# Attention over channels and a routed expert layer on one core: batch 1's k'q moved beside the expert blocks, the first block one step earlier

## The chip, the cores and the metric

The kernel runs on 1 core of a Trainium2 chip. The metric is the device time of one execution in microseconds (us). A core has five engines with instruction queues of their own: TensorE (PE, its weight loads listed as PEld), VectorE (DVE), ScalarE (ACT), GpSimd (POOL) and SyncE (SP, which here issues the loads). The order on each queue is fixed when the program is built.

## The reference

```python
def _attn_ref(q, k, v, tau):              # q, k, v: 4 x 5056 x 256, float32
    qn = q / (np.linalg.norm(q, axis=1, keepdims=True) + 1e-06)
    kn = k / (np.linalg.norm(k, axis=1, keepdims=True) + 1e-06)
    s = kn.transpose(0, 2, 1) @ qn / tau  # 256 x 256 for each batch
    a = softmax of s along its last axis
    return v @ a

def _moe_ref(x, modality_id, w_gate, modality_bias, w1, w2):   # x: 20224 x 256
    logits = x @ w_gate + modality_bias[modality_id]           # 8 experts
    e_idx = np.argmax(logits, axis=1)
    gate_w = softmax(logits) at e_idx
    for e in range(8):
        mask = e_idx == e
        h = np.maximum(x[mask] @ w1[e], 0.0)                   # 256 to 1024
        out[mask] = gate_w[mask, None] * (h @ w2[e])           # 1024 to 256
```

The attention's output, read as 20224 tokens of 256 numbers, is the input of the expert layer. With the reference's inputs three of the eight experts get all tokens: 8704, 1408 and 10112, which are 17, 3 and 20 blocks of 512 rows or less.

## The kernel before

**Stages and steps.** A batch is cut into NS = 10 steps of 512 tokens (the last one is 448). For each batch the kernel first forms the 256 x 256 product k'q and the sums of squares of q and k over all tokens (`kq_pieces`), then the softmax (`softmax_pieces`), then, step by step, v times the attention matrix, the routing, and a scatter of the rows into a DRAM buffer `xs` sorted by expert (`va_pieces`). Blocks of 512 rows of one expert are loaded from `xs` and go through the two expert matrices (`block_pieces`). Batch 0's k'q runs alone at the start. After that there is one loop over g = 0 to 39 (four batches of ten steps). In step g the kernel traces, interleaved piece by piece (`_interleave`): one expert block, if one is due; the v work of step g and the v transposes of step g + 1; and one step of the next batch's k'q.

**k'q.** A step of `kq_pieces` loads 512 rows of q and of k, splits each into a high and a low part (a cast on ACT and a subtraction on DVE, lines 257 and 258) and multiplies: for each of 4 row groups and 2 halves of k's columns a 512-column and a 256-column matmul (lines 283 and 287). The sums of squares come in one of two ways. For steps in the table `SELF` (line 73) TensorE multiplies the part by itself (line 294, tile `selfk` or `selfq`) and the diagonal is taken at the end (line 306, `dg`). For the others ACT squares the rows (line 272) and DVE adds them to `acc` (line 274). Batch 1 has k in `SELF` for steps 0 to 3 and q for none.

**v work and routing.** `tr` transposes v on TensorE (line 460, `vtp`) and splits it (464, 465). `av` does 24 matmuls for each step (line 476, `xp`), and ACT copies the results to `x` (line 480). `route` is a chain of small DVE operations (lines 485 to 533) with three small matmuls in it (`rp`, lines 512 to 514). It yields row numbers `pi`, and POOL issues four scatters for each step (line 407).

**Blocks.** After step g, `slots_by(g)` says how many blocks have been picked. `pick` (a chain of DVE operations on one row) takes an expert with at least 512 rows that are not taken yet. With START = 3 the first pick follows step 3. A block picked after step g runs in step g + LAG, LAG = 4, so the first one runs in step 7. Its weights (w1r and w2r, four loads of 512 KB for each block, lines 615 and 619) wait for the pick, and its rows (`xr`, line 596) for the landing of all scatters up to the step of the pick. Four pieces prepare a block at the end of the step before it: two weight splits (ACT line 634, DVE line 635) and two transposes of its rows (line 645, `xtp`, split by 650 and 651). Then come `hp` matmuls (line 663), the split of h (668, 669) and `y` matmuls (line 683). 40 blocks are run, 33 of them in steps 7 to 39 and the rest after the loop.

**Buffers.** PSUM has eight banks: y0, y1, g0, g1, two `h` and two `aux`. Before the first block (`early`), v's transposes use an `h` bank and y1, and the routing's small matmuls y0. `selfk` and `selfq` hold an `h` bank each while they accumulate. Batch 0's k'q accumulates in y0 and y1. In batch 1, steps 2 to 4 of q and k are loaded into buffers of the expert weights (tags w1r, w2r), the other steps into two buffers of their own.

**Order.** The Tile framework puts the instructions on the queues. It takes priorities from the order in which pieces are traced and uses durations of its own, so that on an engine with nothing due it can place ready work of a much later step. `setup_bias(b)`, traced at the middle of the batch before, is an example: it has a load `modi` on SP behind a memset on POOL (lines 182 and 186).

Of the kernel before, what the change touches and what calls it, by code (L numbers as in the profile page):

```python
# [8 lines left out]
F32 = mybir.dt.float32  # L9
# [9 lines left out]

def _interleave(*streams):  # L20

    lists = [list(s) for s in streams if s]
    total = [len(x) for x in lists]
    at = [0] * len(lists)
    while any(a < n for a, n in zip(at, total)):
        i = min(
            (i for i in range(len(lists)) if at[i] < total[i]),
            key=lambda i: ((at[i] + 0.5) / total[i], i),
        )
        lists[i][at[i]]()  # L30
        at[i] += 1
# [3 lines left out]
def kernel(  # L35
# [14 lines left out]
    P = 128  # L50
    B, N, C = q.shape
    T, D = out.shape
    E, _, FF = w1.shape
    TT = 4
    STEP = P * TT
    NS = -(-N // STEP)
# [14 lines left out]
    LAG = 4  # L71

    SELF = {
        "q": [{1, 4, 7}, set(), set(), set()],
        "k": [set(range(NS)), set(range(4)), set(), set()],
    }
    START = 3

    def parts(s):
        return P if s < NS - 1 else PL  # L80
# [137 lines left out]
    def kq_pieces(b, s):  # L218
        pp = parts(s)
        st = {}  # L220
        t0 = s * STEP

        def load():
            if s == 0:
                gram[b] = [
                    ps1.tile([P, 2 * C], F32, tag=f"{'y' if b == 0 else 'g'}{m}", name=f"g{m}_{b}")
                    for m in range(CH)
                ]
                acc[b] = p1.tile([P, 2, 2 * C], F32, tag="acc", name=f"acc_{b}", bufs=2)
                for n in ("k", "q"):  # L230
                    if SELF[n][b]:
                        selfp[n, b] = ps2.tile([P, CH, 2 * P], F32, tag="h", name=f"self{n}_{b}")
                        norm[n, b] = p1.tile([P, CH], F32, tag=f"n{n}", name=f"n{n}_{b}")
            for n, src, tag in (("q", q, "w1r"), ("k", k, "w2r")):
                if (b == 0 and s % 5 >= 2) or (b == 1 and 2 <= s < START + 2):
                    st[n] = p3.tile([P, TT, C], F32, tag=tag, name=f"{n}_{b}_{s}")
                else:
                    st[n] = p2.tile([P, TT, C], F32, tag=n, name=f"{n}_{b}_{s}")
                rows = src[b, t0 : t0 + pp * TT, :].rearrange("(p t) c -> p t c", t=TT)
                if b == 0 and s == 0:  # L240
                    st[n + "rows"] = rows
                else:
                    nc.sync.dma_start(st[n][:pp], rows)
            if b == 0 and s == 0:
                for h in range(2):
                    ts = slice(2 * h, 2 * h + 2)
                    for n in ("q", "k"):
                        nc.sync.dma_start(st[n][:, ts, :], st[n + "rows"][:, ts, :])

        def split(h):  # L250
            ts = slice(2 * h, 2 * h + 2)
            more = h == 1 and (b == 0 or (b == 1 and s < START + 1))
            qs = p2.tile([P, 2, 2 * C], F32R, tag="xh" if more else "qs", name=f"qs_{b}_{s}_{h}")
            ks = p2.tile([P, 2, 2 * C], F32R, tag="xl" if more else "ks", name=f"ks_{b}_{s}_{h}")
            st[h] = (qs, ks)
            for n, t in (("q", qs), ("k", ks)):
                nc.scalar.copy(t[:pp, :, 0:C], st[n][:pp, ts, :])  # L257
                nc.vector.tensor_tensor(  # L258
                    t[:pp, :, C : 2 * C], st[n][:pp, ts, :], t[:pp, :, 0:C].bitcast(F32), ALU.subtract
                )  # L260
            a = acc[b]
            for n, o in (("q", 0), ("k", C)):
                if s in SELF[n][b]:
                    continue
                first = h == 0 and s == min(set(range(NS)) - SELF[n][b])
                sq = a[:, :, o : o + C]
                if not first:
                    if b == 0 or (b == 1 and s < START + 1):
                        sq = p3.tile([P, 2, C], F32, tag="hh" if n == "q" else "hl", name=f"sq_{b}_{s}_{h}_{n}")
                    else:  # L270
                        sq = p2.tile([P, 2, C], F32, tag="sq", name=f"sq_{b}_{s}_{h}_{n}")
                nc.scalar.activation(sq[:pp], st[n][:pp, ts, :], AF.Square)
                if not first:
                    nc.vector.tensor_tensor(a[:pp, :, o : o + C], a[:pp, :, o : o + C], sq[:pp], ALU.add)  # L274

        def mm(h):
            qs, ks = st[h]
            for t in range(2):
                first = s == 0 and h == 0 and t == 0
                last = s == NS - 1 and h == 1 and t == 1  # L280
                for m in range(CH):
                    g = gram[b][m]
                    nc.tensor.matmul(  # L283
                        g, ks[:pp, t, m * P : (m + 1) * P], qs[:pp, t, :],
                        start=first, stop=False, skip_group_check=True,
                    )
                    nc.tensor.matmul(  # L287
                        g[:, 0:C], ks[:pp, t, C + m * P : C + (m + 1) * P], qs[:pp, t, 0:C],
                        start=False, stop=last, skip_group_check=True,
                    )  # L290
                    for n, x in (("k", ks), ("q", qs)):
                        mine = SELF[n][b]
                        if s in mine:
                            nc.tensor.matmul(  # L294
                                selfp[n, b][:, m, :], x[:pp, t, m * P : (m + 1) * P],
                                x[:pp, t, :].rearrange("p (s c) -> p s c", s=2)[:, :, m * P : (m + 1) * P],
                                start=s == min(mine) and h == 0 and t == 0 and m == 0,
                                stop=s == max(mine) and h == 1 and t == 1,
                                skip_group_check=True,
                            )  # L300
            for n in ("k", "q"):
                if h == 1 and SELF[n][b] and s == max(SELF[n][b]):

                    dg = p1.tile([P, 2 * P], F32, tag="sc", name=f"dg{n}_{b}", bufs=2)
                    for m in range(CH):
                        nc.vector.scalar_tensor_tensor(
                            dg, selfp[n, b][:, m, :], 1.0, ident12, ALU.mult, ALU.mult,
                            accum_out=norm[n, b][:, m : m + 1],
                        )

        yield load
        for h in range(2):
            yield lambda h=h: split(h)
            yield lambda h=h: mm(h)
# [109 lines left out]

    def slots_by(g):

        return max(0, g + 1 - START)

    first_block = LAG + START

    def va_pieces(b, s):
# [20 lines left out]
            st["L"] = p2.tile([P, TT, E], F32, tag="L", name=f"L_{g}")  # L452

        def tr(h):
            if early and h == 1:
                tp = ps1.tile([P, 512], F32, tag="y1", name=f"vtp_{g}_{h}")
            else:
                tp = ps2.tile([P, 512], F32, tag="h" if early else "aux", name=f"vtp_{g}_{h}")
            for t in range(TT):
                nc.tensor.matmul(  # L460
                    tp[:, t * P : (t + 1) * P], st["v"][:, t, h * P : (h + 1) * P], ident,
                    is_transpose=True, start=t == 0, stop=True, skip_group_check=True,
                )
            nc.scalar.copy(st["vh"][:, h, :], tp)
            nc.vector.tensor_tensor(st["vl"][:, h, :], tp, st["vh"][:, h, :].bitcast(F32), ALU.subtract)
# [16 lines left out]
        def route():  # L482
# [22 lines left out]
            ohf = oh.rearrange("p e t -> p (e t)")  # L505
            rtf = run_t.rearrange("p e t -> p (e t)")
            nc.vector.tensor_tensor_scan(rtf, keep, ohf, 0.0, ALU.mult, ALU.add)
            if early:
                rp = ps1.tile([P, 512], F32, tag="y0", name=f"rp_{g}")
            else:  # L510
                rp = ps2.tile([P, 512], F32, tag="aux", name=f"rp_{g}")
# [256 lines left out]
    for g in range(G):  # L768
        b, s = divmod(g, NS)
        streams = []  # L770
        for gg, blk in waiting:
            if gg <= g - LAG + 1:
                once(blk, "load")
        if len(waiting) > 0 and waiting[0][0] <= g - LAG:
            _, blk = waiting.pop(0)
            streams.append(block_stream(blk, waiting[0][1] if waiting and waiting[0][0] <= g - LAG + 1 else None))
        soft = list(softmax_pieces(b)) if s == 0 and b > 0 else []
        streams.append(soft + (va[g + 1][0] if g + 1 < G else []) + va[g][1])
        if b + 1 < B:
            streams.append(list(kq_pieces(b + 1, s)))  # L780
        _interleave(*streams)
        if waiting and waiting[0][0] <= g - LAG + 1:
            once(waiting[0][1], "load")
            once(waiting[0][1], "prep")
        if s == NS // 2 and b + 1 < B:
# [98 lines left out]
```

## Time and profile before

| | us |
|---|---|
| median of 3 runs (range) | 1244.78 (1243.62 to 1246.61) |
| the profiled execution's own time | 1245.85 |
| its span, first to last instruction | 1243.5 |
| PE busy | 1221.7 |
| DVE busy | 843.9 |
| ACT busy | 754.1 |
| POOL busy | 348.7 |

The page gives the busy time of each engine and the chain of work that ended last. For one stretch, the trace is read by windows (busy time of each engine between two moments) and by rows in order of time: start in us, length in us, engine, line, operation, output and input, shapes, count; in brackets the idle time before the row and what ended it. A matmul's length holds its way through the array, so what one costs in a row of many is the distance from its start to the next start. "SPq" is the queue that issues loads.

### The profile page before, as it was taken

Reading aid. Unit: us, or ns where it says so; the run is one execution under the profiler, and the core shown is the slowest. Engines: PE = TensorE matmul, PEld = TensorE weight load, DVE = VectorE, ACT = ScalarE, POOL = GpSimd, SP = SyncE. Lnnn points to the kernel's source line nnn. Section 1 sums busy time; section 2 is a strip of 40 time slices with the busy share of each in tenths; the row PEclk is TensorE's granted clock in tenths of the full one; section 3 lists DMA queues with packets and bytes.
Section 4 is the critical chain, followed back from the end, with each engine's and each line's share of the span. In section 5 each row is a group of like instructions: output and inputs, shape, how many; then the busy total and the mean of one; then the engine's idle time right before and its main releaser. Section 6 shows DMA issues by size and latency. Waiting matters only on the chain.

```text
span 1243.5 us, 23786 instructions
## 1 busy us (share of the span) xinstructions
PE 1221.7 (98%) x8316; PEld 1116.2 (90%) x8316; DVE 843.9 (68%) x2215; ACT 754.1 (61%) x1531; POOL 348.7 (28%) x348
## 2 busy tenths in 40 slices
PE   8998999999999999999999999999999999999997
PEld 6897899999999999999999999999999999999997
DVE  7898967777777666866776776566655666665552
ACT  7885866666666666766666665565555555545553
POOL 0036343132222222322222222222332222321121
PEclk9998999999999999999999999999999999999999
DMA  9758864555555555555555554444554443467320
GB/s 322 252 191 282 271 205 151 161 190 186 176 170 172 178 171 171 162 176 170 170 181 186 175 167 136 136 134 143 164 173 154 149 153 121 147 211 219 119 95 28
DMA packets 113026, 215.06 MB, mean 173 GB/s; under 512 B 16128, under 2 KB 61696, under 8 KB 112896
## 3 DMA queue, kind: packets, MB, share of 16 engines
q1 hardware_dynamic: 97632, 171.84, 44.3%
q0 software_dynamic: 15264, 41.60, 8.8%
q8 instruction: 67, 1.10, 0.4%
q14 instruction: 63, 0.52, 0.1%
HBM read 167.06 MB, written 46.34 MB: 172 GB/s over the span
## 4 chain that ended last, share of the span: by engine, by line
PE 90%; DVE 3%; issue 3%; DMA 2%; ACT 1%; POOL 1%; SPq 0%; POOLq 0%; DVEq 0%; ACTq 0%
PE y L683 33%; PE hp L663 33%; PE xp L476 9%; PE g L283 5%; PE g L287 3%; PE vtp L460 3%; PE xtp L645 2%; DMA q<-in_q_dram 1%; PE selfk L294 1%; DVE acc L274 1%; POOL out_dram L407 1%; DMA xs<-x,pi 0%; PE ns L329 0%; DVE qs L258 0%; DVE w2l L635 0%
## 5 line engine op out<-in xcount | busy, mean ns | idle before, releaser
L683 PE MATMUL y<-w2h,hh 128*128 128x256 f32 x1264 | 356.7, 282 | 0.0
L407 POOL DMA_INDIRECT xs<-x,pi x160 | 173.0, 1081 | 647.8 <-ACT w1h L634 483.2
L683 PE MATMUL y<-w2l,hh 128*128 128x256 f32 x1264 | 352.7, 279 | 0.0
L683 PE MATMUL y<-w2h,hl 128*128 128x256 f32 x1264 | 351.4, 278 | 0.0
L669 DVE SCALAR_TENSOR_TENSOR hl<-hp,hh 128x512 fp32r<-128x512 f32 (+1 forms) x320 | 216.2, 676 | 147.0 <-ACT hh L668 146.8
L668 ACT ACTIVATE hh<-hp 128x512 fp32r<-128x512 f32 (+1 forms) x320 | 190.1, 594 | 169.2 <-PE hp L663 167.2
L663 PE MATMUL hp<-xh,w1h 128*128 128x512 f32 (+1 forms) x640 | 255.8, 400 | 0.3 <-ACT xh L650 0.3
L663 PE MATMUL hp<-xl,w1h 128*128 128x512 f32 (+1 forms) x640 | 250.3, 391 | 0.0
L663 PE MATMUL hp<-xh,w1l 128*128 128x512 f32 (+1 forms) x640 | 249.7, 390 | 0.0
L683 PEld LDWEIGHTS y<-w2h,hh 128*128 128x128 f32 x1264 | 237.5, 188 | 12.0 <-ACT yo L694 0.2
L683 PEld LDWEIGHTS y<-w2l,hh 128*128 128x128 f32 x1264 | 238.1, 188 | 10.0
L683 PEld LDWEIGHTS y<-w2h,hl 128*128 128x128 f32 x1264 | 236.6, 187 | 0.1
L407 POOL DMA_INDIRECT out_dram<-yo,xr x158 | 163.0, 1032 | 157.5 <-ACT yo L694 113.3
L635 DVE TENSOR_TENSOR w2l<-w2r,w2h 128x512 fp32r<-128x512 f32 x160 | 110.2, 689 | 71.9 <-ACT w2h L634 71.9
L635 DVE TENSOR_TENSOR w1l<-w1r,w1h 128x512 fp32r<-128x512 f32 x160 | 109.8, 686 | 55.5 <-ACT w1h L634 55.1
L634 ACT CAST w2h<-w2r 128x512 fp32r<-128x512 f32 x160 | 100.1, 625 | 74.9 <-PE y L683 67.4
L663 PEld LDWEIGHTS hp<-xh,w1l 128*128 128x128 f32 x640 | 120.1, 188 | 26.2
L634 ACT CAST w1h<-w1r 128x512 fp32r<-128x512 f32 x160 | 101.0, 631 | 60.0 <-PE hp L663 55.7
L663 PEld LDWEIGHTS hp<-xl,w1h 128*128 128x128 f32 x640 | 120.5, 188 | 14.1 <-DVE xl L651 0.4
L663 PEld LDWEIGHTS hp<-xh,w1h 128*128 128x128 f32 x640 | 120.1, 188 | 13.6 <-ACT xh L650 0.5
L283 PE MATMUL g<-qs,ks 128*128 128x512 f32 (+1 forms) x320 | 121.4, 402 | 5.7 <-ACT ks L257 5.7
L476 PE MATMUL xp<-ah,vh 128*128 128x264 f32 x320 | 96.9, 303 | 0.0
(152 smaller groups left out, 1833.0 us busy)
## 6 DMA issues: line engine op xcount, KB each, us to landing
w1r<-in_moe_w_dram SPq DMA_DIRECT2D x80, 512.0 KB, 3.5
w2r<-in_moe_w_dram SPq DMA_DIRECT2D x80, 512.0 KB, 3.7
xr<-xs SPq DMA_DIRECT2D x38, 516.0 KB, 4.7
v<-in_v_dram SPq DMA_DIRECT2D x36, 512.0 KB, 5.3
q<-in_q_dram SPq DMA_DIRECT2D x35, 512.0 KB, 7.5
k<-in_k_dram SPq DMA_DIRECT2D x35, 512.0 KB, 9.8
xs<-pad SPq DMA_DIRECT2D x9, 516.0 KB, 5.6
xs<-x,pi POOLq DMA_INDIRECT x160, 5.1
```

The lines of the kernel that those rows point to most:

```text
L283: nc.tensor.matmul(g, ks[:pp, t, m * P : (m + 1) * P], qs[:pp, t, :], start=first, stop=False, skip_group_check=True,)
L287: nc.tensor.matmul(g[:, 0:C], ks[:pp, t, C + m * P : C + (m + 1) * P], qs[:pp, t, 0:C], start=False, stop=last, skip_group_check=True,)
L407: ins = nc.gpsimd.indirect_dma_start(out=dst, out_offset=bass.IndirectOffsetOnAxis(ap=idx, axis=0), in_=rows, in_offset=None, bounds_check ...
L460: nc.tensor.matmul(tp[:, t * P : (t + 1) * P], st["v"][:, t, h * P : (h + 1) * P], ident, is_transpose=True, start=t == 0, stop=True, skip ...
L476: nc.tensor.matmul(xp[:, 0:DE], a[:, h, t * P : (t + 1) * P], w[:, h, :], start=i == 0, stop=i == len(seq) - 1,)
L634: nc.scalar.copy(hi, src)
L635: nc.vector.tensor_tensor(lo, src, hi.bitcast(F32), ALU.subtract)
L645: nc.tensor.matmul(tp[:, t * P : (t + 1) * P], st["xr"][:, t, h * P : (h + 1) * P], identr, is_transpose=True, start=t == 0, stop=True, sk ...
L663: nc.tensor.matmul(hp[:, 0:rows], w[:, h, fs], x[:, h, 0:rows], start=i == 0, stop=i == len(seq) - 1)
L668: nc.scalar.activation(hh[:, 0:rows], hp[:, 0:rows], AF.Relu)
L669: nc.vector.scalar_tensor_tensor(hl[:, 0:rows], hp[:, 0:rows], 0.0, hh[:, 0:rows].bitcast(F32), ALU.max, ALU.subtract)
L683: nc.tensor.matmul(y, a[:, tsl], w[:, j % 2, :], start=(j == 0 and i == 0 and t % 2 == 0), stop=(j == NJ - 1 and i == 2), skip_group_check ...
```

## The change

Four edits belong together.

- **Plan of k'q.** Batch 1's k'q is no longer one step in each of steps 0 to 9 but follows `PLAN`: steps 0, 1, 2 as before, none in 3 to 5, step 3 in step 6, and 4 and 5, 6 and 7, 8 and 9 in pairs in steps 7, 8 and 9. Other batches keep one in each step.
- **Sums of squares of batch 1.** q's go through TensorE in steps 0 to 2 (before: never), k's in steps 0 to 2 (before: 0 to 3). The conditions for borrowed buffers follow `AHEAD = 3`.
- **First block.** START is 2, so the first pick follows step 2 and the first block runs in step 6. At step 12 (`SKIP`) no pick is made, and from step 16 on a block runs 3 steps after its pick, so that each of steps 6 to 39 has one block. 34 blocks run in steps, one more than before. From the eleventh block on, the picks follow the same steps as before.
- **PSUM.** In steps 0 to 2 v's transposes use y0 and y1, and the routing's small matmuls an `aux` bank, since `selfk` and `selfq` now hold both `h` banks.

```diff
-    lists = [list(s) for s in streams if s]
+    lists = [list(s) for s in streams if len(s) > 0]
...
-        "q": [{1, 4, 7}, set(), set(), set()],
-        "k": [set(range(NS)), set(range(4)), set(), set()],
+        "q": [{1, 4, 7}, set(range(3)), set(), set()],
+        "k": [set(range(NS)), set(range(3)), set(), set()],
     }
-    START = 3
+    START = 2
+
+    PLAN = [[0], [1], [2], [], [], [], [3], [4, 5], [6, 7], [8, 9]]
+    SKIP = 12
+    AHEAD = 3
...
-                if (b == 0 and s % 5 >= 2) or (b == 1 and 2 <= s < START + 2):
+                if (b == 0 and s % 5 >= 2) or (b == 1 and 2 <= s < AHEAD):
                     st[n] = p3.tile([P, TT, C], F32, tag=tag, name=f"{n}_{b}_{s}")
...
-            more = h == 1 and (b == 0 or (b == 1 and s < START + 1))
+            more = h == 1 and (b == 0 or (b == 1 and s < AHEAD))
...
-                    if b == 0 or (b == 1 and s < START + 1):
+                    if b == 0 or (b == 1 and s < AHEAD):
...
-        return max(0, g + 1 - START)
+        return max(0, g + 1 - START - (g >= SKIP))
+
+    def lag(g):
+
+        return LAG if g < SKIP + LAG else LAG - 1
...
-            if early and h == 1:
+            if g < AHEAD:
+                tp = ps1.tile([P, 512], F32, tag=f"y{h}", name=f"vtp_{g}_{h}")
+            elif early and h == 1:
                 tp = ps1.tile([P, 512], F32, tag="y1", name=f"vtp_{g}_{h}")
             else:
                 tp = ps2.tile([P, 512], F32, tag="h" if early else "aux", name=f"vtp_{g}_{h}")
...
-            if early:
+            if early and g >= AHEAD:
                 rp = ps1.tile([P, 512], F32, tag="y0", name=f"rp_{g}")
...
-            if gg <= g - LAG + 1:
+            if gg <= g + 1 - lag(g + 1):
                 once(blk, "load")
-        if len(waiting) > 0 and waiting[0][0] <= g - LAG:
+        if len(waiting) > 0 and waiting[0][0] <= g - lag(g):
             _, blk = waiting.pop(0)
-            streams.append(block_stream(blk, waiting[0][1] if waiting and waiting[0][0] <= g - LAG + 1 else None))
+            streams.append(block_stream(blk, waiting[0][1] if waiting and waiting[0][0] <= g + 1 - lag(g + 1) else None))
...
         if b + 1 < B:
-            streams.append(list(kq_pieces(b + 1, s)))
+            steps = PLAN[s] if b == 0 else [s]
+            streams.append([f for i in steps for f in kq_pieces(b + 1, i)])
         _interleave(*streams)
-        if waiting and waiting[0][0] <= g - LAG + 1:
+        if waiting and waiting[0][0] <= g + 1 - lag(g + 1):
             once(waiting[0][1], "load")
             once(waiting[0][1], "prep")
```

## The prediction

> **What bounds the kernel now.** The page first: engine totals, then the chain that ended last.
>
> ```profile
> span 1243.5 us, 23786 instructions
> PE 1221.7 (98%) x8316; PEld 1116.2 (90%) x8316; DVE 843.9 (68%) x2215; ACT 754.1 (61%) x1531; POOL 348.7 (28%) x348
> PE 90%; DVE 3%; issue 3%; DMA 2%; ACT 1%; POOL 1%; SPq 0%; POOLq 0%; DVEq 0%; ACTq 0%
> ```
>
> TensorE is the chain. A change can gain only where TensorE waits or runs slowly, so I cut the span at the places where it does (stretch, its length, then busy us of PE, PEld, DVE, ACT, POOL, granted clock, DMA share, GB/s).
>
> ```profile
> 55.00:103.00 48.00, 47.20 (x350) 43.59 (x348) 44.87 (x160) 37.34 (x89) 18.61 (x19) 1.00 0.59 191
> 103.00:116.00 13.00, 8.53 (x48) 7.63 (x46) 8.82 (x42) 8.83 (x20) 9.29 (x8) 0.74 0.98 308
> 116.00:150.00 34.00, 33.10 (x218) 29.02 (x219) 32.21 (x89) 23.85 (x50) 7.91 (x9) 1.00 0.91 305
> 150.00:1180.00 1030.00, 1029.81 (x7029) 940.57 (x7028) 687.23 (x1786) 616.63 (x1248) 294.61 (x284) 1.00 0.52 166
> ```
>
> From 150 to 1180 us TensorE is never idle, and nothing there can be won by order. The change rearranges 55 to 150 us, where batch 1's k'q runs beside steps 0 to 9. The hole is at 103 us, in TensorE's order of time (start, length):
>
> ```profile
> 102.98 0.28 PE L287 MATMUL g<-qs,ks 128*128 128x256 f32 x1
> 107.39 0.21 PE L512 MATMUL rp<-oh,trim 128*128 128x32 bf16 x1 [4.14 <-DVE pki L579]
> 108.94 0.42 PE L476 MATMUL xp<-ah,vl 128*128 128x264 f32 x1
> 109.16 0.42 PE L476 MATMUL xp<-ah,vh 128*128 128x264 f32 x1
> 112.45 0.56 PE L283 MATMUL g<-qs,ks 128*128 128x512 f32 x1
> 112.98 0.29 PE L476 MATMUL xp<-al,vh 128*128 128x264 f32 x1
> 113.10 0.28 PE L476 MATMUL xp<-ah,vl 128*128 128x264 f32 x1
> 114.75 0.81 PE L645 MATMUL xtp<-identr,xr 128*128 128x128 f32 x8
> 115.89 0.73 PE L663 MATMUL hp<-xh,w1h 128*128 128x512 f32 x2 [0.33 <-ACT xh L650]
> ```
>
> Idle for 4.1 us; then from 107.4 to 112.5 the xp matmuls start 0.22 us apart instead of 0.12, so about 2.5 us of these 5.1 are lost to a clock at half. The first block's matmuls begin at 115.9. What held TensorE, and what feeds the block, stands in ACT's, SP's and POOL's rows (and the last row, from the chain of waits):
>
> ```profile
> 104.90 0.62 ACT L634 CAST w1h<-w1r 128x512 fp32r<-128x512 f32 x1 [4.11 <-DMA w1r<-in_moe_w_dram]
> 96.23 0.38 SPq L186 DMA_DIRECT2D modi<-in_moe_modality_id_dram  x1
> 98.88 0.41 SPq L615 DMA_DIRECT2D w1r<-in_moe_w_dram  x1
> 109.29 0.35 SPq L596 DMA_DIRECT2D xr<-xs  x1
> 79.90 1.19 POOL L407 DMA_INDIRECT xs<-x,pi  x1 [34.73 <-ACT sq_q L272]
> 94.64 1.38 POOL L407 DMA_INDIRECT xs<-x,pi  x1 [0.30 <-issue]
> 95.99 0.21 POOL L182 MEMSET modi<- 128x80 int32 x1
> 103.02 0.97 POOL L407 DMA_INDIRECT xs<-x,pi  x1 [0.30 <-issue]
> 103.02 5.84 DMA xs<-x,pi
> ```
>
> Two chains end here. ACT stood on a weight split whose load SP had issued only at 98.9, and with it stood the copies that free TensorE's banks. And the block's rows: 16 scatters (four steps of four) run on POOL nearly end to end from 79.9 to 103.0, the last lands at 108.9, the load of xr goes out at 109.3, the transposes come at 114.8. The rest of steps 0 to 6 ends at the same 114.75: in the kernel of before the rows come just in time.
>
> **The change, part by part.** Unit costs of TensorE are distances between starts:
>
> ```profile
> 55.39 0.28 PE L294 MATMUL selfk<-ks 128*128 128x256 f32 x1
> 55.51 0.40 PE L283 MATMUL g<-qs,ks 128*128 128x512 f32 x1
> 55.74 0.28 PE L287 MATMUL g<-qs,ks 128*128 128x256 f32 x1
> 93.24 1.04 PE L460 MATMUL vtp<-ident,v 128*128 128x128 f32 x8
> 94.04 0.37 PE L476 MATMUL xp<-ah,vh 128*128 128x264 f32 x1
> ```
>
> 0.12 for 256 columns, 0.23 for 512, 0.12 for an xp, 0.80 for eight v transposes. One k'q step has eight of each g form: 8 x 0.35 = 2.8 us; a v step 24 x 0.12 + 0.8 + 0.1 = 3.8.
>
> *Sums of squares.* q gains three steps of eight 256-column matmuls, k loses one (range(4) to range(3)): 16 x 0.12 = +1.9 us of TensorE, the only work that is added to the bounding engine. In exchange ACT loses the squares and DVE the additions of q in three steps. Two more diagonal reductions on DVE (q's, about 0.4 us each as k's) and one tiny add in the norms lie under the block.
>
> *Pick one step earlier.* The first pick follows step 2, so xr waits for 12 scatters and not 16. By the rows the 12th starts 14.7 us after the first, against 23.1 for the 16th, in which 2.6 us of bias work on POOL are included. The first scatter can move too: DVE's route of step 0 is stretched by additions.
>
> ```profile
> L274 DVE TENSOR_TENSOR acc<-acc,sq_q 128x512 f32<-128x512 f32 x11 | 7.6, 687 | 0.0
> 73.76 0.68 DVE L274 TENSOR_TENSOR acc<-acc,sq_q 128x512 f32<-128x512 f32 x1
> 74.36 0.18 DVE L493 SCALAR_TENSOR_TENSOR val<-lm,desc 128x32 f32<-128x32 f32 x1
> 78.76 0.20 DVE L528 TENSOR_REDUCE pi<-pos 128x4 int32<-128x32 f32 x1
> DMA to landing us min/median/max: 2.8/3.2/6.1
> ```
>
> One addition holds DVE 0.60 us; four stand between this route's start (72.3) and its row numbers (78.8), all for steps that no longer square in this way. 4 x 0.6 = 2.4 us, so the first scatter at 77.5. Bounds: 79.9 (another split takes their place) and 74.7 (a fifth addition in softmax is gone too, and v's split of the next steps lies behind). Landing: 5.8 by the critical scatter, 3.2 by the median of the scatters up to 104 us; I take 4.5. Load of xr to first hp as now: 115.9 - 108.9 = 7.0. So the first block begins at 77.5 + 14.7 + 4.5 + 7.0 = **103.7 us**, 12.2 sooner; bounds 99.6 and 107.4.
>
> *k'q moved.* What the block no longer has in front of it: k'q of steps 3 to 6 (4 x 2.8 = 11.2) and step 6's own v work (3.8), together 15.0 us. It comes later at full rate, where TensorE has no hole. With nothing of it done ahead, the end moves by -12.2 + 15.0 = +2.8: the block is ready sooner than TensorE's work shrinks. But the planner pulls ready work forward: the modi load at 96.2 is the third batch's (a step-15 item). Step 3's k'q, queued for step 6, has its two buffers free after step 0, so I let it fill the gap whole: -2.8. Bounds: nothing, or steps 3 and 4 and the v work, 9.4. Net 0.0.
>
> *The clock.* TensorE's gap before 103.7 is then some 6 us in pieces that I can't place. In one piece it brings the slow stretch again, 2.5 us, now on top; in short pieces none. I take half: **+1.2**. The only row is one 4.1 us gap, followed by half rate. The Trainium skill (TensorE: Matmul & The Clock Gate, Part 1: The HAM clock gate) says that the clock falls to half after an idle window of about 3.4 us and returns after about as long busy; the slow stretch here was 5.1 us. By that rule two gaps of 3 us would leave the clock up and the sum at 0.0, one of 6 would make it +2.5.
>
> *Other edits.* v's transposes of steps 0 to 2 in y0 and y1: these banks held batch 0's k'q, whose last reader is in softmax ahead of them on TensorE; at most the 1.3 us wait already seen there comes again. The tiles of k'q step 3 on ordinary buffers: nothing, they are loaded long ahead; if not, ACT's wait on a q load, 2.6 us once in 116 to 150. The skip at step 12 and the shorter lag give slots 10 to 39 the same picks as before, one step earlier run, with a whole step (29.8 us, below) still between pick and load. The tail loses one block and the steps gain one, in both places TensorE is full.
>
> *Pairs.* Steps 7 to 9 carry a second k'q. A step with block and k'q, and one without k'q:
>
> ```profile
> 203.31:233.14 29.83, 29.75 (x204) 27.21 (x205) 23.24 (x63) 22.11 (x44) 8.25 (x8) 1.00 0.54 175
> 865.70:892.71 27.01, 27.01 (x188) 24.81 (x189) 16.20 (x45) 14.68 (x31) 8.47 (x8) 1.00 0.50 157
> ```
>
> The pair makes it 32.6 us with some 5 more on DVE (eight operations of 0.60) and about as much on ACT: 28 of 32.6 even for this step, which holds a softmax. No cost while q and k loads arrive; they have two buffers each, and SP's queue (v, weights, xr) is ahead of them.
>
> **Sum.** -12.2 + 15.0 - 2.8 + 1.2 = +1.2 us. On the profiled execution's own 1245.85 (span 1243.5, 2.35 around it) that is 1247.05; this run is 1.07 above the median 1244.78, so **1246.0** against the median.
>
> **Rivals.**
> *The gap is filled (faster).* Steps 3 and 4 of k'q are done before the block, rows land in 3.2 us, ACT meets its weights in time. Then 5.6 us are pulled ahead instead of 2.8, the block begins at 77.5 + 14.7 + 3.2 + 7.0 = 102.4 and the clock stays: -13.5 + 15.0 - 5.6 = -4.1, 1240.7. For it: the planner's reach, both buffers free, and DVE relieved of three steps of eight operations of 0.60, 14 us, before the block. Against: in its order of before k'q followed the steps as written once softmax was past. Floor: all idle (6.0 us in 55 to 150) and slow clock (2.5) gone, 1.9 paid, -6.6, 1238.2.
> *TensorE starves (slower).* ACT's queue again reaches the first w1h split before its load has landed. Place: L634 ahead of x copies and v casts. Now less lies in front of it, while the load is still issued behind the bias's modi load, which waits for POOL's memset behind the twelfth scatter: 77.5 + 14.7 = 92.2, then 2.7 from modi to w1r (96.2 to 98.9) and 6.0 to landing (98.9 to 104.9), 101. Every us from ACT's arrival to 101 that no k'q covers is lost; it decides as soon as ACT arrives before 97. With nothing pulled ahead and the slow clock in full: +2.8 + 2.5 = +5.3, 1250.1; with the bounds 107.4 and none pulled ahead +9.0, 1253.8.
> *Pairs collide.* A q load in steps 7 to 9 is late behind blocked weight loads: 2.6 us as in ACT's rows above, twice, on top of the sum, +6.4, 1251.2. Against: TensorE rode over those waits without idling.
> *A pick comes too early and takes an empty block*, about 23 us. From the routing in the reference's data: the fullest expert has 788 rows at the first pick and 569 at the tightest (step 11), against 512 needed. It does not happen.
>
> **Chances.** Forecast 0.40, its own range 1242 to 1249; filled 0.32; starved 0.22; pairs 0.06. Differences of 0.2% (2.5 us) are what a measurement here can tell. Faster: 0.30 of filled and 0.02 of the forecast's edge, 0.32; slower: starved 0.22, pairs 0.06 and 0.05 of the edge, 0.33; the same: the rest, 0.35. Range 1240.0 to 1252.0: the cases near the floor and the worst starvation are left out, some 0.1 each.
>
> **What would show it.** First xr load near 97 instead of 109.3, first hp near 104; TensorE idle 5 to 8 us in 55 to 110; 24 selfq matmuls and no q additions before it; TensorE again without idle from the block on, and the end section unchanged. Wrong if the first scatter stays at 79.9, if ACT's wait on w1r is longer than 4.1 us, if k'q of steps 4 and 5 runs ahead of the block, or if steps 7 to 9 show idle.

## The result

| | before | after |
|---|---|---|
| median of 6 runs (range), us | 1245.09 (1243.62 to 1246.61) | 1251.15 (1248.74 to 1255.47) |
| the profiled execution's own time | 1245.85 | 1248.74 |
| its span | 1243.5 | 1246.5 |

The ratio of the medians is 1.0053, interval [1.0038, 1.0068]: slower by half a per cent, by 6 us in the medians and 2.9 in the two profiled executions. The traces can speak for the 2.9 only; the profiled execution after is the fastest of its six, and what the others lose on top has no trace.

The page of the kernel after, its totals and the engines' shares of the chain that ended last:

```profile
span 1246.5 us, 23848 instructions
PE 1226.0 (98%) x8332; PEld 1118.5 (90%) x8332; DVE 844.5 (68%) x2216; ACT 756.4 (61%) x1527; POOL 350.3 (28%) x348
PE 91%; issue 3%; DMA 2%; DVE 2%; ACT 1%; POOL 1%; SPq 0%; POOLq 0%; ACTq 0%; DVEq 0%
```

TensorE is still the chain. The same stretches as in the prediction, of the kernel after (stretch, length, busy us of PE, PEld, DVE, ACT, POOL, clock, DMA share, GB/s):

```profile
55.00:103.00 48.00, 45.80 (x319) 40.25 (x318) 42.68 (x134) 36.94 (x84) 16.51 (x18) 1.00 0.66 216
103.00:116.00 13.00, 9.51 (x61) 8.19 (x59) 10.50 (x54) 9.73 (x24) 7.56 (x8) 0.87 0.96 311
116.00:150.00 34.00, 32.69 (x212) 28.91 (x213) 29.94 (x92) 22.08 (x47) 10.24 (x8) 0.95 0.75 243
150.00:250.00 100.00, 99.13 (x678) 90.45 (x678) 67.87 (x182) 63.27 (x129) 34.84 (x34) 1.00 0.53 175
```

Between 55 and 150 us TensorE idles 7.0 us (2.2 + 3.5 + 1.3), in the kernel before 6.2 (0.8 + 4.5 + 0.9). The one hole at 103 has become many small ones, and the idle time has not shrunk. The rows in order of time show why. First two of the kernel before, the first `xp` of step 1 and the first `rp` of step 0; then those of the kernel after:

```profile
71.21 0.30 PE L476 MATMUL xp<-ah,vh 128*128 128x264 f32 x1
76.39 0.18 PE L512 MATMUL rp<-oh,trim 128*128 128x32 bf16 x1
```

```profile
75.79 0.18 PE L522 MATMUL rp<-oh,trim 128*128 128x32 bf16 x1
75.82 0.37 PE L486 MATMUL xp<-ah,vh 128*128 128x264 f32 x1
85.30 0.19 PE L522 MATMUL rp<-oh,trim 128*128 128x32 bf16 x1
85.34 0.37 PE L486 MATMUL xp<-ah,vh 128*128 128x264 f32 x1
94.75 0.19 PE L522 MATMUL rp<-oh,trim 128*128 128x32 bf16 x1
94.78 0.37 PE L486 MATMUL xp<-ah,vh 128*128 128x264 f32 x1
108.90 0.19 PE L522 MATMUL rp<-oh,trim 128*128 128x32 bf16 x1 [1.19 <-DVE oh L509]
110.26 0.59 PE L486 MATMUL xp<-ah,vh 128*128 128x264 f32 x1 [0.78 <-ACT x L490]
114.64 0.85 PE L655 MATMUL xtp<-identr,xr 128*128 128x128 f32 x8 [0.45 <-ACT x L490]
117.31 1.22 PE L673 MATMUL hp<-xh,w1h 128*128 128x512 f32 x2 [1.82 <-ACT xh L660]
```

In the kernel before, step 1's v work started 5.2 us ahead of step 0's `rp`. Now, three times, the first `xp` of a step starts 0.03 or 0.04 us after the first `rp` of the step before it. `rp` of steps 0 to 2 takes its place in the two `aux` banks, among the `xp` tiles, which use the same two in the order in which they are traced. So v's work of step g + 1 cannot begin until route of step g has got as far as its matmul. The scatters follow that rhythm (the first and the twelfth, and the load of `xr` on SP; the first of step 1 leaves at 88.05, of step 2 at 98.49):

```profile
79.82 1.16 POOL L411 DMA_INDIRECT xs<-x,pi  x1 [7.27 <-ACT x L490]
102.76 0.98 POOL L411 DMA_INDIRECT xs<-x,pi  x1 [0.31 <-issue]
109.15 0.35 SPq L606 DMA_DIRECT2D xr<-xs  x1
```

The twelfth scatter leaves at 102.76, in the kernel before at 94.64. The first block waits for twelve scatters instead of sixteen, and still xr is loaded at 109.15, before at 109.29. From that load to the first `hp` it takes 8.2 us, before 6.6: between the transposes at 114.64 and the split of `xtp` at 116.67 ACT works off two weight splits and two casts of k'q. How much of the moved work then stood ahead of the first `hp` is in the groups of TensorE from 50 us to that `hp`; kernel before, then kernel after:

```profile
L283 PE MATMUL g<-qs,ks 128*128 128x512 f32 x56 | 22.1, 412 | 0.0
L476 PE MATMUL xp<-ah,vh 128*128 128x264 f32 x56 | 17.5, 316 | 0.0
```

```profile
L287 PE MATMUL g<-qs,ks 128*128 128x512 f32 x60 | 22.6, 401 | 0.2
L486 PE MATMUL xp<-ah,vh 128*128 128x264 f32 x48 | 14.9, 314 | 2.0 <-ACT x L490 1.1 <-DVE pm L582 0.6 <-DVE pos L532 0.3
L298 PE MATMUL selfq<-qs 128*128 128x256 f32 x24 | 6.9, 296 | 0.0
```

Eight of each make a step: 7 steps of k'q before, 7.5 after, though the plan writes three; 7 steps of v before, 6 after.

**A ledger.** TensorE is full from the block on, so the end moves by how much later the first `hp` starts, plus the work that stood ahead of it before and no longer does (2.8 us for a k'q step, 3.8 for a v step). Here +1.4 - 1.4 + 3.8 = +3.8, against the +2.9 between the executions. The same sum is made for each experiment below. It is a way of keeping accounts: it says how much, not what caused it.

### The profile page after: what moved, and what is told of

Its sections match the earlier page's. It is cut to its first block, busy times and chain, and to the rows that moved or that the text cites. A ratio compares the mean times of both kernels' runs of the same rounds, so it can differ in the third digit from the quotient of the medians.

```text
span 1246.5 us, 23848 instructions
## 1 busy us (share of the span) xinstructions
PE 1226.0 (98%) x8332; PEld 1118.5 (90%) x8332; DVE 844.5 (68%) x2216; ACT 756.4 (61%) x1527; POOL 350.3 (28%) x348
## 4 chain that ended last, share of the span: by engine, by line
PE 91%; issue 3%; DMA 2%; DVE 2%; ACT 1%; POOL 1%; SPq 0%; POOLq 0%; ACTq 0%; DVEq 0%
PE hp L673 34%; PE y L693 34%; PE xp L486 9%; PE g L287 5%; PE g L291 3%; PE vtp L470 3%; PE xtp L655 2%; DMA q<-in_q_dram 1%; DMA k<-in_k_dram 1%; PE selfk L298 1%; DVE acc L278 1%; POOL out_dram L411 1%; PE ns L333 0%; DMA w1r<-in_moe_w_dram 0%; PE selfq L298 0%
## 5 line engine op out<-in xcount | busy, mean ns | idle before, releaser
L673 PEld LDWEIGHTS hp<-xh,w1h 128*128 128x128 f32 x640 | 120.5, 189 | 15.0 <-ACT xh L660 2.0
```

Source lines behind the costliest of these rows:

```text
L673: nc.tensor.matmul(hp[:, 0:rows], w[:, h, fs], x[:, h, 0:rows], start=i == 0, stop=i == len(seq) - 1)
```

## The experiments

The time is a ratio to runs of the kernel before on the same chip. The table has the comparison itself and the runs on two chips on which the kernel before takes 1244 to 1245 us. Six kernels ran on two other chips, called slow chips below, on which the kernel before takes 1285 us and the two kernels that ran on both kinds took 32 and 44 us more; TensorE idled 1.4 to 2.4% there even between 250 and 1180 us, and some waits of ACT are put down to "remote". Intervals are 0.5 to 0.6% wide there, and one ratio did not hold elsewhere (below). Times from these slow chips are given, but decide nothing.

| run | first hp | k'q / v steps ahead of it | ledger | own time against 1245.85 | ratio [interval] |
|---|---|---|---|---|---|
| after | 117.31 | 7.5 / 6 | +3.8 | +2.9 | 1.0053 [1.0038, 1.0068] |
| banks back (e1) | 106.19 | 4.5 / 6 | +1.1 | +4.4 | 1.0047 [1.0033, 1.0061] |
| before, rp in aux (e2) | 127.35 | 8 / 7 | +8.7 | +6.6 | 1.0081 [1.0067, 1.0094] |
| no q squares, banks back (e3) | 108.74 | 4.25 / 6 | +4.4 | +8.2 | 1.0047 [1.0034, 1.0061] |
| plan one each (e5) | 117.23 | 7.5 / 6 | +3.7 | +2.7 | 1.0029 [1.0015, 1.0042] |
| earlier block alone (f2b) | 118.77 | 6 / 6 | +9.5 | +9.4 | 1.0060 [1.0047, 1.0074] |
| q squares alone (f3b) | 121.52 | 7 / 7 | +5.6 | +5.7 | 1.0038 [1.0024, 1.0052] |

Part of these sums has nothing to do with the stretch that is changed. Batch 0's k'q, which runs alone at the start, does not end at the same time in every execution. Its last matmul in the kernel before; then a wait near the start and the last matmul in f3b:

```profile
49.57 0.28 PE L294 MATMUL selfk<-ks 112*128 112x256 f32 x1
```

```profile
14.48 0.50 PE L283 MATMUL g<-qs,ks 128*128 128x512 f32 x1 [3.32 <-ACT ks L257]
52.97 0.28 PE L294 MATMUL selfk<-ks 112*128 112x256 f32 x1
```

f3b is 3.4 us late before the change has begun to act, e3 1.8 (51.40), the other five of the table 0.1 to 0.6. It need not come from the edit: the same kernel ends this stage at different times, that of f3b at 50.03 on a slow chip (52.97 here), that of f2b at 52.32 there (50.03 here). The first `hp`, the ledger and the own time hold it alike, so it has to be taken off all three before they are put down to an edit.

### The banks (e2, e1)

The kernel before with one condition changed:

```diff
-            if early:
+            if early and g >= 3:
                 rp = ps1.tile([P, 512], F32, tag="y0", name=f"rp_{g}")
```

> The kernel before with one edit: the routing's small matmuls of steps 0 to 2 in an aux bank. Theory A: xp of steps 1 to 3 each start only after the rp of the step before, 3 to 5 us each; the scatters of step 3 are issued near 113 (103.0), first hp near 126 (115.9), with one more step of k'q pulled ahead (2.8): 1247 to 1253, slower than before by 2 to 8. Theory B: 1244 to 1246, no difference.

1254.58 us. `rp` and the `xp` behind it follow each other as in the changed kernel (85.89 and 85.93, 98.52 and 98.55). The window around its first `hp`:

```profile
120.00:130.00 10.00, 4.23 (x18) 3.44 (x19) 8.80 (x35) 4.18 (x10) 5.22 (x5) 0.51 1.06 346
```

This edit alone costs 10 us: the tie between `rp` and `xp` is real and dear. But with the tie taken out of the changed kernel (and both halves of v's transposes in y1, since y0 is now the routing's) little or no time came back:

```diff
             if g < AHEAD:
-                tp = ps1.tile([P, 512], F32, tag=f"y{h}", name=f"vtp_{g}_{h}")
+                tp = ps1.tile([P, 512], F32, tag="y1", name=f"vtp_{g}_{h}")
...
-            if early and g >= AHEAD:
+            if early:
                 rp = ps1.tile([P, 512], F32, tag="y0", name=f"rp_{g}")
```

> The changed kernel with the routing's small matmuls of steps 0 to 2 back in y0, and both halves of v's transposes of these steps in y1. Theory A (banks): with rp in an aux bank, the xp of step g+1 can't begin before the route of step g has reached its rp, so the v steps are slowed to the pace of the route chain and the first block comes late. Then here xp of step 1 starts within 2 us of the end of xp of step 0 (4.5 us in the changed kernel), the 12th scatter is issued near 93 us (102.8), the first hp comes at 104 to 109 (117.3), and the time falls to 1243 to 1248 (1251.2). Theory B (the planner's appetite: k'q is pulled ahead of the block whatever the banks are): seven or more steps of k'q still stand before the first hp, first hp after 114, time 1249 to 1252.

1250.23 us. TensorE's rows, and the windows:

```profile
104.79 1.23 PE L655 MATMUL xtp<-identr,xr 128*128 128x128 f32 x8 [3.59 <-DMA xr<-xs]
106.19 1.22 PE L673 MATMUL hp<-xh,w1h 128*128 128x512 f32 x2 [0.17 <-ACT xh L660]
231.74 0.19 PE L522 MATMUL rp<-oh,trim 112*128 112x32 bf16 x1 [1.80 <-DVE oh L509]
```

```profile
95.00:105.00 10.00, 5.42 (x39) 4.60 (x37) 7.93 (x43) 7.00 (x17) 7.52 (x7) 0.96 1.01 320
130.00:150.00 20.00, 19.20 (x132) 17.23 (x131) 14.66 (x44) 11.88 (x26) 7.93 (x8) 1.00 0.51 158
150.00:200.00 50.00, 49.36 (x331) 44.30 (x330) 37.80 (x96) 33.49 (x68) 10.02 (x9) 1.00 0.54 175
200.00:250.00 50.00, 48.09 (x322) 43.37 (x320) 36.63 (x98) 35.56 (x74) 18.51 (x19) 1.00 0.57 189
```

First scatter at 76.04 and first `hp` at 106.19, as theory A said; the time it gave for that, 1243 to 1248, was missed. But only 4.5 steps of k'q had been pulled ahead: the block came 9.7 us sooner with 10.8 us less in front of it, and TensorE waited for the rows. Another 3.3 us are idle from 130 to 250. So in the changed kernel the tie does two things: it delays the rows, and it lets k'q fill the time that it makes. What the single bank for both transposes costs by itself was not run; TensorE's longest wait on a transpose's copy there is 0.95 us.

### The earlier block alone (f2b), and what holds it (f5)

START, SKIP and lag as in the change; banks, sums of squares (k in steps 0 to 3, q never) and one k'q step in each step as before. AHEAD stays 3, so that steps 3 and 4 of k'q use ordinary buffers.

```diff
-        "q": [{1, 4, 7}, set(range(3)), set(), set()],
-        "k": [set(range(NS)), set(range(3)), set(), set()],
+        "q": [{1, 4, 7}, set(), set(), set()],
+        "k": [set(range(NS)), set(range(4)), set(), set()],
...
-    PLAN = [[0], [1], [2], [], [], [], [3], [4, 5], [6, 7], [8, 9]]
+    PLAN = [[s] for s in range(NS)]
```

On a slow chip first:

> The first block one step earlier and nothing else: the kernel before's banks, its sums of squares (k in steps 0 to 3, q never on TensorE) and one step of k'q in each step. Ahead of the first block stand six steps of k'q and six of v in place of seven and seven: 6.6 us of TensorE less. Starvation theory: first scatter at 79 to 80 as before, the twelfth 13 to 15 us later, first hp at 105 to 108; 8 to 10 us sooner with 6.6 us less to do leaves 2 us of gain at most, and the gap ahead of the block brings the slow clock (2.5): 1243 to 1247, no difference that can be told. If an earlier first block were the gain it looks like (one block more inside the loop), it would show here alone, under 1242.

1284.75 us, 1.0005 [0.9977, 1.0033]. Then on one of the others:

> The first block one step earlier alone, a second time, since the first time every kernel on that chip, the kernel before too, stood in waits that the trace puts down to another core or an unknown queue (up to 5 us at a time in 95 to 105 us), and the interval was 0.55% wide. Starvation theory: first scatter 80, first hp 105 to 108, TensorE idle 5 to 8 us between 95 and 108 and the slow clock behind it, 1243 to 1247. Earlier-is-better theory: under 1242.

1253.19 us, +8. Both theories missed: the part that should gain loses 8 us. The trace shows where, in rows of DVE, POOL, SP, ACT and PE:

```profile
90.17 0.15 DVE L587 CAST pki<-pk 1x2 int32<-1x2 f32 x1
98.48 0.19 POOL L186 MEMSET modi<- 128x80 int32 x1
98.70 0.39 SPq L190 DMA_DIRECT2D modi<-in_moe_modality_id_dram  x1
100.16 0.41 SPq L623 DMA_DIRECT2D w1r<-in_moe_w_dram  x1
105.34 0.62 ACT L642 CAST w1h<-w1r 128x512 fp32r<-128x512 f32 x1 [10.87 <-DMA w1r<-in_moe_w_dram]
106.29 1.11 PE L468 MATMUL vtp<-ident,v 128*128 128x128 f32 x4 [9.66 <-ACT x L488]
```

The pick is known at 90.2. SP has the load of modi ahead of w1r; that load waits for a memset on POOL, which stands behind the twelfth scatter (at 97.52). So w1r goes out at 100.2, ACT stands on it for 10.9 us with the copies of x behind, and TensorE for 9.7, followed by half clock:

```profile
95.00:105.00 10.00, 1.63 (x12) 1.26 (x10) 0.27 (x3) 0.00 (x0) 6.96 (x8) 0.84 0.58 142
105.00:115.00 10.00, 7.71 (x31) 6.71 (x32) 7.95 (x35) 7.23 (x17) 0.50 (x1) 0.50 0.91 320
```

To test it, the memset moves to VectorE, in this kernel and in the kernel before:

```diff
-        nc.gpsimd.memset(modi, 0)
+        nc.vector.memset(modi, 0)
```

> The first block one step earlier alone, as before, with one further edit: the memset of modi is on VectorE in place of POOL, so that the load of modi on SP no longer waits behind the scatters, and the loads of the first weights no longer wait behind that load. In the kernel without this edit TensorE stood 9.7 us for a copy of x, ACT 10.9 us for w1r, and w1r was issued at 100.2, 1.5 after modi at 98.7, though the pick was known at 90.3. Queue theory (the 8 us that the earlier block cost are the weights' place on SP's queue): w1r issued at 90 to 92, ACT's wait under 3 us, TensorE's 9.7 gone, the slow clock with it, first hp at 108 to 112, and 1242 to 1246. Work theory (too little of TensorE's work is ahead of the rows, whatever the weights do): the wait moves to the rows (xtp on xr), 5 us or more, and 1249 to 1253.

> The kernel before with the memset of modi on VectorE and nothing else. There ACT stood 4.1 us for w1r at 104.9, TensorE 4.1 us at 103 and 2.5 us at a slow clock. Queue theory: w1r issued about 3 us sooner or more, ACT's wait gone, up to 4 us of TensorE's hole with it; the rows (last scatter at 103, load of xr at 109.3) then set the block, so 1240 to 1244. Work theory: the hole is the rows', 1244 to 1246.

Both fell on a slow chip: 1282.48 us, 0.9996 [0.997, 1.0022], and 1286.45, 1.0003 [0.9974, 1.0031]. No gain is measured. The order in the trace of f5 is what the queue theory asks for:

```profile
93.38 0.13 DVE L587 CAST pki<-pk 1x2 int32<-1x2 f32 x1
94.55 0.41 SPq L623 DMA_DIRECT2D w1r<-in_moe_w_dram  x1
111.08 0.72 PE L671 MATMUL hp<-xh,w1h 128*128 128x512 f32 x2 [0.33 <-ACT xh L658]
```

w1r follows the pick by 1.2 us instead of 10, and ACT's wait for it is gone. The nearest comparison is f2, the same kernel without this edit on the other slow chip: there w1r followed the pick by 6.4 us, ACT stood 1.4 us for it and the first `hp` came at 116.86. In f5 it comes at 111.08 behind the same six steps of k'q and of v, 5.8 sooner, of which 2.6 are batch 0's earlier end. So how the 9.7 us of f2b arise can be read from the order of its rows, and the edit removes that order; that they would come back on the other chips is not shown. Nor is it shown what an earlier block without that stall is worth: against the first `hp` of before, 115.89 on another chip, the ledger of f5 is -4.8 + 2.8 + 3.8 = +1.8, but against b5, a slow chip too (122.67 behind seven steps of each), it is -11.6 + 6.6 = -5.0. In b5 ACT still stood 2.8 us on w1r, because there w1r waited for the pick (pki at 103.89, w1r at 105.13), not for modi.

### The squares (f3b, e3)

The kernel before with q's sums of squares of steps 0 to 2 on TensorE, and, because these need an `h` bank, both halves of v's transposes of those steps in y1:

```diff
-        "q": [{1, 4, 7}, set(), set(), set()],
+        "q": [{1, 4, 7}, set(range(3)), set(), set()],
...
-            if early and h == 1:
+            if g < 3 or (early and h == 1):
```

> The kernel before with q's sums of squares of steps 0 to 2 on TensorE and nothing else but the banks that this needs: v's transposes of steps 0 to 2 both in y1, routing in y0 as before. 24 matmuls of 256 columns more, 2.8 us of TensorE. Banks theory: the first scatter comes at 76 in place of 79.9, the first block some 4 us sooner, and the hole at 103 shrinks by as much: 2.8 paid, up to 4 won, 1243 to 1246. If the single bank y1 for both transposes holds v's work, idle with waits of vtp or xp shows ahead of 100 us, and the time is 1247 or more.

1294.3 us, 1.0073 [1.0042, 1.0104], on a slow chip.

> The kernel before with q's sums of squares of steps 0 to 2 on TensorE and the transposes of those steps both in y1, a second time for the same reason. It came out 0.7% slower there, against an expected -1 to +2 us, with 3.8 us of a wait that the trace cannot name and 4.6 us of waits for the copies of x. If those were the chip's, the time here is 1243 to 1246. If they are the kernel's own (step 6's v work was placed ahead of routing, and 24 matmuls were added), 1250 or more.

1250.01 us, +5. In its trace 3.4 of the 5.7 us are batch 0's late end, and the first scatter, at 83.31 instead of 79.90, is late by just as much. The other 2.2 lie near 95 us (window, and rows of PE and DVE):

```profile
95.00:105.00 10.00, 8.68 (x49) 8.09 (x50) 6.77 (x36) 4.31 (x11) 7.87 (x8) 0.70 0.56 185
94.46 0.45 PE L460 MATMUL vtp<-ident,v 128*128 128x128 f32 x1 [2.63 <-DMA v<-in_v_dram]
94.82 0.18 DVE L194 TENSOR_SCALAR m1i<-modi 128x40 int32<-128x40 int32 x1 [4.85 <-DMA modi<-in_moe_modality_id_dram]
```

24 matmuls (2.8 us) were paid, and the first scatter gained nothing. But here too DVE, with route's operations behind it, stands 4.8 us on a modi load of a later batch, TensorE 2.6 us on a load of v that SP issued behind it (modi at 88.52), and the clock falls (0.50 from 95 to 100 us). So the trace does not give the price of the squares by themselves, and the +5 of the medians has no trace beyond this one. The other way round, the changed kernel without q's squares and with the banks of before:

```diff
-        "q": [{1, 4, 7}, set(range(3)), set(), set()],
+        "q": [{1, 4, 7}, set(), set(), set()],
```

> The changed kernel without q's sums of squares on TensorE (ACT and DVE do them again), with the banks of before (v's transposes in h and y1, rp in y0). Theory A: as with rp in y0, first hp at 104 to 109, and 24 matmuls of 0.12 (2.8 us) less on TensorE; DVE has ten additions more in front of the routes. If TensorE's added work is what counts, 1241 to 1245, 2 to 3 below the kernel with rp in y0 alone. If DVE's relief was worth it, the first scatter is 2 to 3 us later than there and the times are equal. Theory B: 1248 to 1250.

1250.9 us. With less TensorE work ahead of the block it starves: `xtp` waits 4.7 us for xr (another 2.7 us are idle from 150 to 250):

```profile
100.00:110.00 10.00, 2.82 (x14) 2.33 (x15) 4.68 (x24) 3.85 (x8) 7.27 (x7) 0.63 0.82 236
```

### The plan (e5, e4, g0)

The changed kernel with one step of k'q in each step:

```diff
-    PLAN = [[0], [1], [2], [], [], [], [3], [4, 5], [6, 7], [8, 9]]
+    PLAN = [[s] for s in range(NS)]
```

> The changed kernel with batch 1's k'q one step in each step again, all else as changed. Theory A: the plan is not what decides; while xp waits for rp the planner draws the same k'q ahead either way, first hp at 116 to 119, 1250 to 1252 as the changed kernel. Rival P (the plan starves or crowds the early steps): it goes back towards before, 1245 to 1248.

1248.68 us, some 2 us less than the changed kernel in the medians, though the intervals of the two overlap and the profiled executions are equal (1248.55 and 1248.74). The work ahead of the block is the same 7.5 steps: in the changed kernel the planner places k'q the same, whatever the plan writes. What goes is 0.9 us of idle time later, a wait of `rp` on DVE at 230 us (e5, to be compared with the last window of the kernel after):

```profile
150.00:250.00 100.00, 100.00 (x687) 91.42 (x686) 69.54 (x183) 64.56 (x132) 32.88 (x34) 1.00 0.53 177
```

Two more put e1's banks together with other plans, one step each (e4) and `[[0],[1],[2],[3],[4],[5,6],[7],[8],[9],[]]` (g0):

> The changed kernel with the routing's small matmuls back in y0, v's transposes of steps 0 to 2 both in y1, and batch 1's k'q one step in each of steps 0 to 9. In the order that is built, six steps of k'q and six of v stand ahead of the first block; they were 7.5 and 6 in the changed kernel and 4.5 and 6 with the banks alone. Banks theory (what was lost, was lost to the tie between routing and v work): first scatter 76, first hp at 106 to 108; the block comes 8 to 10 us sooner than in the kernel before with 6.6 us of work less in front of it, no idle after 150 us, so 2 us gained less what the slow clock takes: 1243 to 1246. Starvation theory (freeing the banks only uncovers the wait for the rows): TensorE idles 6 us or more between 95 and 107, the clock falls, and the time is that of the kernel before or above, 1246 to 1249.

> The changed kernel with the routing's small matmuls back in y0, v's transposes of steps 0 to 2 both in y1, and k'q of batch 1 one step in each of steps 0 to 4, two in step 5, one in each of steps 6 to 8: so 6.8 steps of k'q stand ahead of the first block instead of 4.5, and no two of them share a step that has a block. Starvation theory: the wait for the rows is covered by what is placed in front of the block. First hp at 107 to 109, TensorE idle under 4 us between 95 and 109, no idle after 150: against the kernel before the block is 8 us sooner with 0.6 of k'q and 3.8 of v less ahead of it, so 2 to 4 us gained, 1240 to 1244. If instead ACT and DVE are the limit there (splits of q and k, copies of x), the added k'q pushes the scatters out and the time stays at 1246 to 1249.

On a slow chip: 1284.19, 0.9996 [0.997, 1.0023], and 1285.47, 1.0011 [0.9987, 1.0034]. First `hp` at 112.73 and 114.54. With these banks the plan does count: 4.5 steps of k'q stand ahead of the block in e1, 6 in e4 and some 6.6 in g0. Neither time is told from the kernel before, and no version was found that beats it.

## Why the prediction was right or wrong

The range (1240.0 to 1252.0) held the time, and the sum came out 5 us low. That the range held was luck: 1251.15 lies outside the forecast's own 1242 to 1249 and beside what two rivals gave (1250.1 and 1251.2), and it came about by neither's mechanism. That the sum came near was luck too, since two large terms failed in opposite directions.

- **Block 12.2 us sooner: wrong.** It came 1.4 us later, 13.6 after the forecast 103.7: 2.3 in the first scatter, 8.2 in the way from there to the twelfth (22.9 us, not 14.7), 3.1 from there to the first `hp` (14.6, not 11.5). The step that failed is "Other edits": it costed v's transposes in y0 and y1, and passed over the other half of the same edit, the routing's matmuls in `aux`. That half alone costs 10 us (e2), and without it the first `hp` is at 106.19 (e1).
- **First scatter at 77.5: wrong in the change, 79.82.** "Four additions less" was a misreading of the rows before. `acc` is added to in the order of the steps, and batch 1's five additions of q for steps 0 to 2 stand at 60.74 to 70.31, all ahead of the route; the four that were counted are three of q's steps 3 and 4 and one of k's step 4, which go on being squared on ACT. In the changed kernel three additions stand between the route's start (72.67) and its row numbers, and with them the four diagonal reductions of `selfk` and `selfq`, which the prediction had put under the block. That it came out at the bound of 79.9 is near its reason, not quite it. The additions on DVE of the kernel after, and the row numbers:

```profile
76.59 0.69 DVE L278 TENSOR_TENSOR acc<-acc,sq_q 128x512 f32<-128x512 f32 x1 [0.69 <-ACT sq_q L276]
77.37 0.69 DVE L278 TENSOR_TENSOR acc<-acc,sq_k 128x512 f32<-128x512 f32 x1
78.07 0.69 DVE L278 TENSOR_TENSOR acc<-acc,sq_q 128x512 f32<-128x512 f32 x1
78.68 0.20 DVE L538 TENSOR_REDUCE pi<-pos 128x4 int32<-128x32 f32 x1
```

- **15.0 us of work no longer in front, one step (2.8) pulled ahead: wrong by size.** 12.2 by the forecast, 2.4 by the counts. The planner pulled 4.5 steps, because the tie opened gaps and k'q was what was ready. Where the banks were free it pulled 1.5 (e1), inside the bound of two that the prediction gave.
- **So -12.2 + 12.2 became +1.4 + 2.4.** The form of the sum was right and holds within 2.1 us in all runs but two. Those two, e1 and e3, idle 3.3 and 2.7 us after the block, which the ledger does not count; with them the gap is at most 1.1.
- **The clock, +1.2: the size was near, the mechanism not.** TensorE ran at half from 110.3 to 113.5 (`xp` 0.22 apart) and from 117.3 to some 120.5 (`hp` 0.43 apart): 3.1 us lost, against 2.5 before, so +0.6. Ahead of each stretch TensorE was not idle in one piece but thinly busy (windows of the kernel after):

```profile
107.00:110.30 3.30, 1.33 (x10) 0.98 (x10) 1.90 (x16) 2.68 (x7) 2.69 (x3) 0.98 1.06 385
113.50:117.30 3.80, 1.53 (x13) 1.21 (x12) 2.29 (x14) 3.78 (x11) 3.04 (x3) 0.95 0.99 344
```

  The longest wait in them is 1.2 and 1.8 us. The Trainium skill (TensorE: Matmul & The Clock Gate, Part 1: The HAM clock gate) has the clock fall after an idle window of about 3.4 us. Read as one idle piece, as the prediction read it, waits of 1.2 and 1.8 us would have left the clock up; here it fell after windows that were 40% busy. The prediction took short pieces as free; in this trace they were not.
- **Squares, +1.9 on TensorE: the count was right (24 `selfq`, 8 `selfk` fewer), the price left out.** The prediction names the 1.9, but its sum has no term for it; only the floor counts it. Alone the edit reads +5 in the medians; its trace leaves 2.2 us after batch 0's late end, with the wait on modi in them (f3b).
- **Pairs at no cost: nearly.** 0.9 us in the changed kernel. The rival's 2.6 us twice did not come (in the kernel before the 2.6 is the sum of two waits, the longer of 1.4), nor its cause: where the block is early, 3.3 us are lost from 130 to 250, and the wait that the trace names there is routing's `rp` on DVE (2.9 us in four), not a q load.
- **"TensorE starves": its mechanism is real.** f2b shows it as the prediction placed it, modi behind the twelfth scatter and w1r behind modi, with 9.7 us instead of 5.3. In the changed kernel it does not act; ACT waits 1.7 us on w1r, which is issued 1.3 us after the pick (pki at 101.39).
- **An empty block** did not occur. The end section, held unchanged, moved a little: from 1180 us on TensorE idles 6.6 us, before 8.5. The 0.9 by which the ledger is above the measured 2.9 may lie there; it was not traced further.

The parts alone cost +8 (block), +5 (squares) and +10 (banks); together +6. They are not added up: each acts on the same stretch, and what already waits for one of them need not lose again by the next. No run takes that apart further.

What stays open: why the runs of the changed kernel spread over 6.7 us (batch 0's end, which varies by up to 3.4, may be part of it), why e1 idles 3.3 us after the block, what the squares cost by themselves, and what e4, g0 and f5 are worth on a chip that is not slow.

## What to carry to other kernels

When one item is moved ahead in a full engine's stream, write down both columns: how much sooner it starts, and how much of that engine's work no longer stands in front of it. The end moves by the difference, and a planner may change both. For a tile that moves to another rotation of buffers, ask whose next tile now waits for it: one tag cost 10 us here, and no instruction was added. Before a difference of a few us is put down to an edit, look whether the two executions were level when the edited stretch began. And before a pick, a load or a weight is advanced, read the queue it is issued from, to the memset behind which a small load of another stage stands.

## What the runs showed of the hardware

- TensorE's granted clock was 0.50 and 0.51, for 3.2 us each time, after stretches of 3.3 and 3.8 us in which TensorE was 40% busy, without a wait over 1.8 us.
- Batch 0's k'q of the same kernel ended up to 2.9 us apart in two executions on two chips (f3b 52.97 and 50.03; f2b 50.03 and 52.32).
- Chips ran the same kernel 3% apart (1245 and 1285). On a slow one the earlier block alone read 1.0005 [0.9977, 1.0033], on another 1.0060 [1.0047, 1.0074]: where a change moves a wait, a ratio from one chip need not hold on the next. On the slow one ACT stood 1.4 us for w1r, not 10.9, and TensorE 5.4 us for routing instead. What makes these chips slow was not traced.
